# A long convolution before two feed-forward layers: spectrum of the signal channel-major, packed signal loads, complex product in fewer operations, b axis of 229 cells

## The chip, the cores and the metric

The kernel runs on one core of a Trainium2 chip. A core has a matrix engine (TensorE, PE in the rows; its weight loads are shown as PEld), three elementwise engines (VectorE, DVE; ScalarE, ACT; GpSimd, POOL) and a queue processor (SyncE, SP), which issues most transfers here. The engines run side by side, each in its own program order, and wait for each other at semaphores. SBUF and PSUM are the memories on the core; a transfer to or from main memory is a DMA. The metric is the device time of one execution in microseconds (us).

## What is computed

```python
h_mlp = np.maximum(pos_emb @ w1, 0.0) @ w2            # 12480 x 128, pos_emb 12480 x 64
h_filt = h_mlp * np.exp(-0.01 * pos)[:, None]
u = x * v                                             # 12480 x 128
L = 2 * S
Uf = np.fft.rfft(u, n=L, axis=1)
Hf = np.fft.rfft(h_filt, n=L, axis=0)
y = np.fft.irfft(Uf * Hf[None, :, :], n=L, axis=1)[:, :S, :]
out = x * y
# then two feed-forward layers, 128 -> 2048 -> 128, on every token:
#   out = square(relu(out @ w_in)) @ w_out
#   out = leaky(out @ w_in2, alpha) @ w_out2
```

S is 12480. All data are 32-bit floats; the weights of the feed-forward layers come as 64-bit words.

## The kernel before

**Index scheme.** The convolution is cyclic, over L = NA x NB = 110 x 227 cells. A position n is written as (a, b) with n = 227 a + 110 b modulo L, so that the Fourier transform falls into one over a (110 values) and one over b (227 values). Both are done as matmuls with tables. Since the signals are real, the a axis gives K2 = 112 rows (cosine and sine of 56 frequencies). On the b axis only 114 columns are kept (HB): b and -b are held side by side and folded into a sum (even part) and a difference (odd part).

**Stages.** Each is a Python generator; `run` interleaves two of them by weights, and every engine executes its own instructions in the order in which they were written. The order is set by hand (`manual_schedule`).

1. `z_stage` and `ar_stage` (L155, L187): filter. Position embeddings are multiplied by w1, windowed, and transformed over a (result `ar`).
2. `u_stage(0)` beside `r_stage` (L333, L207). `r_stage` transforms the filter over b in 28 steps and spills it to main memory, in pieces `r`. `u_stage` treats the 128 channels of the signal in 32 blocks of four (16 for each half h = 0, 1): load x and v, multiply (`mul_xv`, POOL, L247), in seven blocks fold on POOL (L263, L264), transform over a (`u_mm_a`, L273) and, one step later, over b (`u_mm_b`). In half 0 the operands of the b transform are split into a high and a low part, and each product is three matmuls (`mm_b`, L309); in half 1 it is one (L305; an instruction of this kind on 32-bit floats stands twice in the trace). The halves' results are the spectra U.
3. `u_stage(1)` beside `p_stage(0)` (called p0). `p_stage` has 14 steps for each half. A step loads a piece `r`, multiplies it by w2 into the banks H (L384), and forms the complex product with U: four multiplications and a subtraction on DVE (L389, L395) into a buffer T (two in a ring), an addition on POOL (L361) or, in eight of 28 steps, on DVE (L397), and then, one step late (`finish`, L358), the sum and the difference of two channel halves, written back over U on POOL (L364; once for each half on DVE).
4. `p_stage(1)` (called q0) beside `b_stage(0)`; then `b_stage(1)` alone, beside 60 steps that decode feed-forward weights. `b_stage` transforms back over b: per channel one matmul with a column of U as stationary operand (L410), per four channels a copy on ACT (L416) into `gv`.
5. `y_stage` (L427): back over a, multiplied by x; 30 column groups; beside it goes the decoding of weights.
6. `moe` (L614): both feed-forward layers in 25 chunks of up to 500 columns.

**Layout.** U of half 0 lies in the upper halves of the rows of a large buffer G, U of half 1 in R2: `uview` (L114) gives [114 partitions, 112 frequencies k, 128 channels x], with the channels contiguous. So a column of U for one channel (`U[:, :, x]`, L410) steps over 256 floats in G and 128 in R2. The rings for x (eight), v (two) and intermediate results lie in the lower halves of G's rows. x and v are loaded with both signs of b, 110 x 8 x 128 floats a block each (440 KB), `load_x` and `load_v` on SP's queue.

**Order on the queues.** POOL executes, in the order written, per step of u_stage `mul_xv(k + 4)`, `fold(k + 2)`, per step of p_stage the additions and `finish` of the step before. SP issues the loads of x and v, the spills and loads of `r`, the loads of x for y_stage and the weight words, in the order written.

## Time and profile before

| | |
|---|---|
| runs, us | 1514.84, 1514.22, 1513.73 (median 1514.22) |
| span of the profiled execution, us | 1510.0 |
| instructions | 23069 |
| TensorE busy, share of the span | 98% |
| DVE, ACT, POOL busy | 78%, 65%, 59% |
| mean granted TensorE clock | 0.993 |
| moved by DMA | 83.38 MB |

The span runs from the first to the last instruction of the profiled execution; its time outside the span is not recorded, and the runs' median is 4.2 us longer than the span. Busy shares are means over stages with different limits, and a busy TensorE is not one at its peak, since its matmuls are pipelined and their ends are modelled. So a stage is read from its own window: which engine is busy throughout, which waits end last, and how fast the instructions follow each other in the chain.

### The profile page before, as it was taken

Reading aid. Unit: us, or ns where it says so; the run is one execution under the profiler, and the core shown is the slowest. Engines: PE = TensorE matmul, PEld = TensorE weight load, DVE = VectorE, ACT = ScalarE, POOL = GpSimd, SP = SyncE. Lnnn points to the kernel's source line nnn. Section 1 sums busy time; section 2 is a strip of 40 time slices with the busy share of each in tenths; the row PEclk is TensorE's granted clock in tenths of the full one; section 3 lists DMA queues with packets and bytes.
Section 4 is the critical chain, followed back from the end, with each engine's and each line's share of the span. In section 5 each row is a group of like instructions: output and inputs, shape, how many; then the busy total and the mean of one; then the engine's idle time right before and its main releaser. Section 6 shows DMA issues by size and latency. Waiting matters only on the chain.

```text
span 1510.0 us, 23069 instructions
## 1 busy us (share of the span) xinstructions
PE 1476.9 (98%) x7676; PEld 1276.9 (85%) x7676; DVE 1177.1 (78%) x1898; ACT 978.8 (65%) x1887; POOL 898.0 (59%) x808
## 2 busy tenths in 40 slices
PE   8998799999999999999999999999999999999998
PEld 8987689999988888888888888888888888888887
DVE  5987998745878877777777777777777777777998
ACT  5353122243288877777777777777777777777776
POOL 0575886623476666656666666566666656665564
PEclk9998999999999999999999999999999999999999
DMA  8788862224940000000000000000000000000000
GB/s 256 176 241 228 203 168 62 77 52 120 278 134 22 1 1 8 8 8 8 7 1 7 8 7 8 7 8 8 0 8 8 7 8 8 8 1 7 15 14 14
DMA packets 86082, 83.38 MB, mean 55 GB/s; under 512 B 5642, under 2 KB 77642, under 8 KB 85578
## 3 DMA queue, kind: packets, MB, share of 16 engines
q1 hardware_dynamic: 84865, 77.68, 18.5%
q0 software_dynamic: 688, 3.93, 0.8%
q8 instruction: 60, 0.98, 0.3%
q14 instruction: 60, 0.49, 0.1%
q10 hardware_dynamic: 409, 0.29, 0.1%
HBM read 65.03 MB, written 16.86 MB: 54 GB/s over the span
## 4 chain that ended last, share of the span: by engine, by line
PE 88%; DMA 7%; DVE 2%; POOL 2%; issue 1%; ACT 0%; SPq 0%; POOLq 0%; DVEq 0%; ACTq 0%
PE bank L621 24%; PE bank L620 24%; PE bank L622 24%; PE bank L410 7%; DMA G<-in_vs_dram 3%; PE bank L384 3%; DMA r<-spill 3%; PE bank L461 2%; PE bank L460 2%; DVE R L197 2%; PE bank L273 1%; DMA G<-in_pos_dram 1%; POOL G L247 1%; PE bank L305 1%; PE bank L162 1%
## 5 line engine op out<-in xcount | busy, mean ns | idle before, releaser
L673 POOL TENSOR_TENSOR g<-R,g 128x500 fp32r<-128x500 f32 (+1 forms) x598 | 641.6, 1087 | 412.3 <-ACT g L662 306.5
L655 DVE SCALAR_TENSOR_TENSOR R<-bank,e 128x500 f32<-128x500 f32 (+1 forms) x800 | 527.3, 673 | 159.1 <-ACT e L643 118.7
L662 ACT CAST g<-R 128x500 fp32r<-128x500 f32 (+1 forms) x800 | 461.8, 604 | 15.9 <-DVE R L655 13.6
L640 ACT ACTIVATE e<-bank 128x500 f32<-128x500 f32 (+1 forms) x400 | 235.2, 588 | 176.1 <-PE bank L622 174.9
L645 DVE TENSOR_SCALAR e<-bank,alpha 128x500 f32<-128x500 f32 (+1 forms) x266 | 195.6, 735 | 68.5 <-PE bank L622 65.8
L621 PE MATMUL bank<-g,w_o 128*128 128x500 f32 (+1 forms) x400 | 155.5, 389 | 0.2 <-POOL g L673 0.2
L621 PE MATMUL bank<-x,w_i 128*128 128x500 f32 (+1 forms) x400 | 155.4, 389 | 0.0
L622 PE MATMUL bank<-g,w_o 128*128 128x500 f32 (+1 forms) x400 | 155.2, 388 | 0.0
L622 PE MATMUL bank<-x,w_i 128*128 128x500 f32 (+1 forms) x400 | 155.1, 388 | 0.0
L620 PE MATMUL bank<-x,w_i 128*128 128x500 f32 (+1 forms) x400 | 155.0, 388 | 0.0
L620 PE MATMUL bank<-g,w_o 128*128 128x500 f32 (+1 forms) x400 | 154.9, 387 | 0.0
L673 DVE TENSOR_TENSOR g<-R,g 128x500 fp32r<-128x500 f32 (+1 forms) x202 | 149.5, 740 | 0.3 <-ACT g L662 0.3
L621 PE MATMUL bank<-g,w_o0b 128*128 128x500 f32 (+1 forms) x350 | 136.3, 389 | 0.0
L620 PE MATMUL bank<-g,w_o0b 128*128 128x500 f32 (+1 forms) x350 | 135.4, 387 | 0.0
L622 PE MATMUL bank<-g,w_o0b 128*128 128x500 f32 (+1 forms) x350 | 135.3, 387 | 0.0
L247 POOL TENSOR_TENSOR G<-G 110x912 f32<-110x912 f32 x32 | 68.7, 2149 | 81.8 <-DMA G<-in_vs_dram 71.9
L642 ACT ACTIVATE e<-bank 128x500 f32<-128x500 f32 (+1 forms) x134 | 79.1, 590 | 46.2 <-PE bank L622 46.1
L643 ACT ACTIVATE e<-e,alpha 128x500 f32<-128x500 f32 (+1 forms) x134 | 95.6, 714 | 4.4
L416 ACT COPY G<-bank 112x456 f32<-112x456 f32 x63 | 33.9, 539 | 85.3 <-PE bank L410 85.3
L620 PEld LDWEIGHTS bank<-x,w_i 128*128 128x128 f32 x400 | 75.1, 188 | 15.8
L621 PEld LDWEIGHTS bank<-g,w_o 128*128 128x128 f32 x400 | 75.2, 188 | 15.7 <-POOL g L673 0.6
L620 PEld LDWEIGHTS bank<-g,w_o 128*128 128x128 f32 x400 | 75.2, 188 | 15.5
(141 smaller groups left out, 2802.9 us busy)
## 6 DMA issues: line engine op xcount, KB each, us to landing
G<-in_xs_dram SPq DMA_DIRECT2D x32, 440.0 KB
...
```

The costliest lines, as they stand in the source:

```text
L247: nc.gpsimd.tensor_tensor(out=x, in0=x, in1=v, op=ALU.mult)
L410: nc.tensor.matmul(p[:, d], lhsT=U[:, :, e * DH + g * DG + d], rhs=icosb if e == 0 else sinb)
L620: nc.tensor.matmul(p, lhsT=wl, rhs=xh, start=first, stop=False)
L621: nc.tensor.matmul(p, lhsT=wh, rhs=xl, start=False, stop=False)
L622: nc.tensor.matmul(p, lhsT=wh, rhs=xh, start=False, stop=last)
L640: nc.scalar.activation(out=r, in_=p, func=ACTF.Relu)
L642: nc.scalar.activation(out=r, in_=p, func=ACTF.Relu, scale=-1.0)
L643: nc.scalar.activation(out=r, in_=r, func=ACTF.Copy, scale=alpha[:, t:t + 1])
L645: nc.vector.tensor_scalar(out=r, in0=p, scalar1=0.0, scalar2=alpha[:, t:t + 1], op0=ALU.min, op1=ALU.mult)
L655: nc.vector.scalar_tensor_tensor(out=g, in0=p, scalar=0.0, in1=r, op0=ALU.max, op1=op)
L662: nc.scalar.copy(out=gh, in_=g)
L673: eng.tensor_tensor(out=gl, in0=g, in1=gh.bitcast(F32), op=ALU.subtract)
```

## The change

- The b axis has 229 cells (L = 110 x 229), 115 columns are kept, tables have 116. With this number no cell is taken by both signs of b.
- x and v are loaded packed: one array of 112 x 4 x 128 floats a block each (229 KB), in which cells of positive b lie forward and cells of negative b backward. `prep` (POOL) multiplies x by v and then takes the positive part out with a mask (`plus`); `minus` (POOL) subtracts it and reads the rest back to front. Rings: seven for x and v, three for the negative part.
- `u_mm_a` always folds after the transform; the split into high and low parts is gone in both halves; the frequency axis is ordered with cosine and sine alternating (c fastest).
- U is kept with the channels slow and the 112 frequencies contiguous. U of half 0 lies in two pieces (16 channels in the lower halves of G's rows, 112 in the upper).
- In `p_stage` a bank H holds [channel, sign, q, r]; one multiplication (two in half 0, by the pieces) forms U times H for both parts by reading H twice over, into T = (A, B); A of the real part minus B on DVE; A of the imaginary part plus B on POOL, in all steps; then sum and difference on POOL.
- `b_stage` reads a channel's 112 frequencies contiguously.
- Output and y_stage have exactly 12480 columns; four small tables move to the pool `late`, and `xt_first` to the pool `wo`.

```diff
 
 S, D, F, FF = 12480, 128, 64, 2048
-NA, NB = 110, 227
...
 K2 = 2 * KA
 HB = (NB + 1) // 2
-HP = HB // 2
+HP = -(-HB // 2)
+HX = 2 * HP
 KP = KA // 2
...
+    def U(h, x0, n):
+        if h:
+            return R2[:HB].rearrange("p (x k) -> p x k", k=K2)[:, x0:x0 + n]
+        if x0 < XF:
+            return gap[0][:HB, x0:x0 + n, 128 - K2:128]
+        return gap[1][:HB, x0 - XF:x0 - XF + n, 0:K2]
+
+    def parts(h):
+        return [(0, D)] if h else [(0, XF), (XF, D - XF)]
+
+    NX, NM = 7, 3
+    at = [XF]
+
+    def rows(n):
+        at[0] += n
+        assert at[0] <= HX
+        return gap[0][:, at[0] - n:at[0]]
+
+    m_ring = [rows(DG)[:, :, 0:HB] for _ in range(NM)]
+    a_ring = [rows(2 * DG)[:, :, 0:K2] for _ in range(2)]
+    ap_ring = [rows(DG)[:, :, 0:K2] for _ in range(2)]
+    t_ring = [rows(DG)[:, :, 0:K2] if i else gap[1][:, D - XF:D - XF + DG, 0:K2] for i in range(2)]
+    assert at[0] <= HP
+    at[0] = HP
+    x_ring = [[rows(DG) for _ in range(2)] for _ in range(NX)]
...
             if g in z_loads:
-                load_x(z_loads[g][0])
-                load_v(z_loads[g][1])
+                load(z_loads[g])
+                prep(z_loads[g] - 1)
...
+    z_loads = {5: 0, 10: 1, 15: 2, 19: 3, 24: 4, 28: 5}
...
-                    nc.tensor.matmul(p[s][:, j], lhsT=rv[:, f0 + j, :, s], rhs=dfa)
+                    nc.tensor.matmul(p[s][:, j], lhsT=rv[:, f0 + j, :, s], rhs=dfa_f)
...
+            load(NX - 1)
+            prep(NX - 2)
...
-    def load_x(n):
+    loaded, ready = [0], [0]
+
+    def load(n):
         while loaded[0] <= min(n, 2 * NG - 1):
             k = loaded[0]
-            nc.sync.dma_start(out=x_ring[k % NX][:NA], in_=xs[:, k])
+            for t, src in zip(x_ring[k % NX], (xs, vs)):
+                nc.sync.dma_start(out=t[:NAP], in_=src[:, k])
             loaded[0] += 1
 
-    def load_v(n):
-        while loaded[1] <= min(n, 2 * NG - 1):
-            k = loaded[1]
-            if k >= NV:
-                mul_xv(k - NV)
-            nc.sync.dma_start(out=v_ring[k % NV][:NA], in_=vs[:, k])
-            loaded[1] += 1
-
-    def mul_xv(n):
-        while mulled[0] <= min(n, 2 * NG - 1):
-            k = mulled[0]
-            x, v = x_ring[k % NX][:NA, :, 0:HB], v_ring[k % NV][:NA, :, 0:HB]
+    def prep(n):
+        while ready[0] <= min(n, 2 * NG - 1):
+            k = ready[0]
+            x, v = (t[:NA] for t in x_ring[k % NX])
+            x, v = x[:, :, 0:W], v[:, :, 0:W]
+            m = plus.unsqueeze(1).to_broadcast([NA, DG, W])
             nc.gpsimd.tensor_tensor(out=x, in0=x, in1=v, op=ALU.mult)
-            mulled[0] += 1
-
-    z_loads = {0: (0, -1), 6: (0, 0), 11: (1, 0), 15: (1, 1), 20: (2, 2), 25: (3, 3), 28: (4, 4)}
+            nc.gpsimd.tensor_tensor(out=v, in0=x, in1=m, op=ALU.mult)
+            ready[0] += 1
+
+    def minus(k):
+        if k < 2 * NG:
+            x, v = (back_to_front(t[:NA]) for t in x_ring[k % NX])
+            nc.gpsimd.tensor_tensor(out=m_ring[k % NM][:NA], in0=x, in1=v, op=ALU.subtract)
+
+    def back_to_front(t):
+        v = t[:, :, 1:W]
+        st = [list(x) for x in v.ap]
+        st[-1][0] = -st[-1][0]
+        return bass.AP(tensor=v.tensor, offset=v.offset + HB - 1, ap=st)
...
     def u_mm_a(k):
-        x = x_ring[k % NX].rearrange("p (d s) b -> p s d b", s=2)[:NA, :, :, 0:HB]
-        ap = ap_ring[k % 2]
+        u = x_ring[k % NX][1][:NA, :, 0:HB], m_ring[k % NM][:NA]
...
-                nc.tensor.matmul(p[s][:, d], lhsT=lhs[:, d], rhs=dfa)
...
-        ap = ap[:HB, :, 0:K2]
-        nc.scalar.copy(out=ap, in_=p[0])
-        dst = [p[e] if split and lo_engine(k, e) is nc.vector else a[:, e] for e in range(2)]
...
+                nc.tensor.matmul(p[s][:, d], lhsT=u[s][:, d], rhs=dfa)
+        a = a_t[k] = a_ring[k % 2][:HB].rearrange("p (e d) k -> p e d k", e=2)
+        t = ap_ring[k % 2][:HB]
+        nc.scalar.copy(out=t, in_=p[0])
...
+            nc.vector.tensor_tensor(out=a[:, e], in0=t, in1=p[1], op=op)
...
     def u_mm_b(k):
         h, g = divmod(k, NG)
-        U = uview(h)
         a = a_t.pop(k)
         po = bank(r_b, HB, DG, 2, KA)
-        pe = bank(r_b, HB, DG, 2, KA)
-        mm_b(po[:, :, 0], "nsin", a, 1, slice(KA, K2))
-        mm_b(po[:, :, 1], "sin", a, 1, slice(0, KA))
-        t = t_ring[k % 2][:HB, :, 0:K2]
-        nc.scalar.copy(out=t, in_=po.rearrange("p d c k -> p d (c k)"))
-        mm_b(pe.rearrange("p d c k -> p d (c k)"), "cos", a, 0, slice(0, K2))
+        pe = bank(r_b, HB, DG, K2)
+        ao = a[:, 1].rearrange("p d (k c) -> p d k c", c=2)
+        nc.tensor.matmul(po[:, :, 0], lhsT=nsinb, rhs=ao[:, :, :, 1])
+        nc.tensor.matmul(po[:, :, 1], lhsT=sinb, rhs=ao[:, :, :, 0])
+        t = t_ring[k % 2][:HB]
+        nc.scalar.copy(out=t.rearrange("p d (k c) -> p d k c", c=2), in_=po.rearrange("p d c k -> p d k c"))
+        nc.tensor.matmul(pe, lhsT=cosb, rhs=a[:, 0])
+        u = U(h, 2 * DG * g, 2 * DG).rearrange("p (d s) k -> p d s k", s=2)
         for s, op in ((0, ALU.add), (1, ALU.subtract)):
-            x0 = s * DH + g * DG
-            nc.vector.tensor_tensor(
-                out=U[:, :, x0:x0 + DG],
-                in0=pe.rearrange("p d c k -> p (c k) d"),
-                in1=t.rearrange("p d k -> p k d"),
-                op=op,
-            )
+            nc.vector.tensor_tensor(out=u[:, :, s], in0=pe, in1=t, op=op)
 
     def u_stage(h):
         for k in range(h * NG, (h + 1) * NG + 1):
             if k == 0:
-                fold(0)
-                fold(1)
+                minus(0)
+                minus(1)
             if k < (h + 1) * NG:
-                load_x(k + NX - 1)
-                load_v(k + min(NX, XE + 1 + k) - 1)
-                mul_xv(k + 4)
+                load(k + NX - 1)
                 u_mm_a(k)
-                fold(k + 2)
+                minus(k + 2)
+                prep(k + NX - 3)
             if k > h * NG:
                 u_mm_b(k - 1)
             yield
 
     nj = KP // 2
-    add_dve = {nj - 1} | set(range(nj + 1, 2 * nj, 2))
     p_order = [(j + nj - 3) % nj for j in range(nj)]
     p_order += [(j + nj - 6) % nj for j in range(nj)]
 
     def p_stage(h, t_ring, r_ring):
-        U = uview(h)
-        Uc = U.rearrange("p (c k) x -> p c k x", c=2)
         late = []
 
-        def finish(n, j, T):
+        def finish(n, j, A, B):
             last = n % nj == nj - 1
-            if n not in add_dve:
-                nc.gpsimd.tensor_tensor(out=T[:, 1], in0=T[:, 1], in1=T[:, 2], op=ALU.add)
-            for s, op in ((0, ALU.add), (1, ALU.subtract)):
-                eng = nc.vector if last and s == 0 else nc.gpsimd
-                eng.tensor_tensor(
-                    out=Uc[:, :, 4 * j:4 * j + 4, s * DH:(s + 1) * DH],
-                    in0=T[:, 0:2, :, 0],
-                    in1=T[:, 0:2, :, 1],
-                    op=op,
-                )
+            nc.gpsimd.tensor_tensor(out=A[:, :, :, 1], in0=A[:, :, :, 1], in1=B[:, :, :, 0], op=ALU.add)
+            for x0, m in parts(h):
+                y = A[:, x0:x0 + m].rearrange("p (d s) k c -> p d s (k c)", s=2)
+                u = U(h, x0, m).rearrange("p (d s) k -> p d s k", s=2)[:, :, :, 8 * j:8 * j + 8]
+                for s, op in ((0, ALU.add), (1, ALU.subtract)):
+                    eng = nc.vector if last and s == 0 else nc.gpsimd
+                    eng.tensor_tensor(out=u[:, :, s], in0=y[:, :, 0], in1=y[:, :, 1], op=op)
...
-            H = [bank(r_h, HB, 2, 2, 2, DH) for c in range(2)]
             T = t_ring()
             for c in range(2):
-                for s in range(2):
-                    for q in range(2):
+                H = bank(r_h, HB, DH, 2, 2, 2)
+                for q in range(2):
+                    for s in range(2):
                         nc.tensor.matmul(
-                            H[c][:, s, q], lhsT=r[:, q, 2 * s + c], rhs=w2_sb[:, h * 2 * DH:(h + 1) * 2 * DH]
+                            H[:, :, s, q], lhsT=r[:, q, 2 * s + c], rhs=w2_sb[:, h * D:(h + 1) * D]
                         )
-                hv = H[c].rearrange("p s q r d -> p (q r) s d")
-                for uc in range(2):
+                hv = H.rearrange("p d s q r -> p (d s) (q r)")
+                for x0, m in parts(h):
                     nc.vector.tensor_tensor(
-                        out=hv if uc * c else T[:, uc + c + (uc > c)],
-                        in0=U[:, uc * KA + 4 * j:uc * KA + 4 * j + 4].rearrange("p k (s d) -> p k s d", s=2),
-                        in1=hv,
+                        out=T[:, c, x0:x0 + m],
+                        in0=U(h, x0, m)[:, :, 8 * j:8 * j + 8].rearrange("p x (k c) -> p x k c", c=2),
+                        in1=hv[:, x0:x0 + m].unsqueeze(3).to_broadcast([HB, m, 4, 2]),
                         op=ALU.mult,
                     )
-            nc.vector.tensor_tensor(out=T[:, 0], in0=T[:, 0], in1=hv, op=ALU.subtract)
-            if n in add_dve:
-                nc.vector.tensor_tensor(out=T[:, 1], in0=T[:, 1], in1=T[:, 2], op=ALU.add)
+            A, B = T[:, 0], T[:, 1]
+            nc.vector.tensor_tensor(out=A[:, :, :, 0], in0=A[:, :, :, 0], in1=B[:, :, :, 1], op=ALU.subtract)
             if late:
                 late.pop()()
-            late.append(lambda n=n, j=j, T=T: finish(n, j, T))
+            late.append(lambda n=n, j=j, A=A, B=B: finish(n, j, A, B))
...
-                p = bank(r_y if alone else r_ab, K2, DG, HB)
+                p = bank(r_y if alone else r_ab, K2, DG, HX)
                 for d in range(DG):
-                    nc.tensor.matmul(p[:, d], lhsT=U[:, :, e * DH + g * DG + d], rhs=icosb if e == 0 else sinb)
+                    nc.tensor.matmul(
+                        p[:, d], lhsT=U(h, 2 * (g * DG + d) + e, 1)[:, 0], rhs=icosb if e == 0 else isinb
+                    )
...
             late = st.enter_context(tc.tile_pool(name="late", bufs=1))
+            w2_sb = late.tile([128, 2 * D], F32, name="w2_sb")
+            dfa = late.tile([NA, K2], F32, name="dfa")
+            dfa_f = late.tile([NA, K2], F32, name="dfa_f")
+            plus = late.tile([NA, W], F32, name="plus")
...
+            with tc.tile_pool(name="rt", bufs=1) as rt:
+                run((u_stage(0), NG + 1), (r_stage(rt, r_ring), KP))
             big = st.enter_context(tc.tile_pool(name="tt", bufs=1))
-            tt = ring_of(big, 2, [HB, 3, 4, 2, DH], F32, "T")
+            tt = ring_of(big, 2, [HB, 2, D, 4, 2], F32, "T")
             p0, q0 = p_stage(0, tt, r_ring), p_stage(1, tt, r_ring)
             run((u_stage(1), NG + 1), (p0, nj + 1))
...
-        ys = y_stage(wst.tile([128, 3 * HA], F32, name="xt_first"))
-        next(ys)
         with tc.tile_pool(name="wo", bufs=1) as wo:
+            ys = y_stage(wo.tile([128, 3 * HA], F32, name="xt_first"))
+            next(ys)
...
+    packed = np.full((NAP, 128), S)
+    packed[:NA, :HB] = np.where(live[:, :, 0], n[:, :, 0], S)
+    turned, there = n[:, :0:-1, 1], live[:, :0:-1, 1]
+    assert not (live[:, 1:, 0] & there).any()
+    packed[:NA, 1:HB] = np.where(there, turned, packed[:NA, 1:HB])
+    plus = np.zeros((NA, W), np.float32)
+    plus[:, :HB] = live[:, :, 0]
+
     def sig(x):
-        c = np.zeros((NA, D, 2, 128), x.dtype)
-        c[..., :HB] = cells(x).transpose(0, 3, 2, 1)
-        return c.reshape(NA, D // DG, DG * 2, 128)
+        c = np.concatenate([x, np.zeros((1, x.shape[1]), x.dtype)])[packed]
+        return np.ascontiguousarray(c.transpose(0, 2, 1)).reshape(NAP, D // DG, DG, 128)
```

## Rows read from the trace of the kernel before

**Rows 1.** The page: the chain that ended last, by line

```profile
PE bank L621 24%; PE bank L620 24%; PE bank L622 24%; PE bank L410 7%; DMA G<-in_vs_dram 3%; PE bank L384 3%; DMA r<-spill 3%; PE bank L461 2%; PE bank L460 2%; DVE R L197 2%; PE bank L273 1%; DMA G<-in_pos_dram 1%; POOL G L247 1%; PE bank L305 1%; PE bank L162 1%
```

**Rows 2.** Windows by stage: length, busy us (instructions), granted clock, DMA share, GB/s

```profile
62.00:149.30 87.30, 77.37 (x626) 74.08 (x627) 71.06 (x135) 40.67 (x91) 54.60 (x34) 0.94 0.85 229
149.30:240.60 91.30, 79.46 (x577) 69.99 (x576) 86.05 (x131) 17.57 (x33) 76.51 (x55) 0.96 0.66 161
240.60:314.20 73.60, 73.60 (x465) 73.60 (x466) 50.99 (x80) 16.72 (x31) 43.37 (x34) 0.98 0.25 72
314.20:364.20 50.00, 49.54 (x259) 49.41 (x258) 18.12 (x43) 22.38 (x49) 11.68 (x16) 1.00 0.18 54
364.20:418.70 54.50, 54.42 (x457) 53.99 (x457) 46.81 (x111) 11.63 (x32) 24.64 (x34) 1.00 0.90 267
418.70:1510.00 1091.30, 1086.28 (x4798) 900.14 (x4797) 857.68 (x1350) 842.74 (x1558) 672.62 (x625) 1.00 0.03 12
```

**Rows 3.** Lines by form on POOL, 62 to 149.3 us

```profile
L247 POOL TENSOR_TENSOR G<-G 110x912 f32<-110x912 f32 x17 | 36.6, 2150 | 32.5 <-DMA G<-in_vs_dram 28.3 <-PE bank L213 3.9
```

**Rows 4.** The chain in order of time: start us, us, what (instructions)

```profile
65.90 1.24 PE bank L309 x9
...
75.46 1.79 PE bank L213 x16
...
197.87 1.60 PE bank L273 x16
199.46 1.51 PE bank L305 x6
...
220.47 1.75 PE bank L384 x16
...
252.07 3.07 PE bank L410 x16
```

**Rows 5.** Lines by form, first 430 us, weight loads: busy us, mean ns

```profile
L273 PEld LDWEIGHTS bank<-dfa,G 110*114 110x114 f32 x512 | 57.4, 189 | 1.1 <-issue 0.7 <-DVE a_lo L284 0.2 <-POOL G L364 0.2
...
L410 PEld LDWEIGHTS bank<-dfb,G 114*112 114x112 f32 x256 | 50.3, 285 | 2.2 <-issue 2.2
...
L460 PEld LDWEIGHTS bank<-ide,G 112*128 112x128 f32 x228 | 35.8, 196 | 0.0
```

**Rows 6.** Lines by form on POOL, 149.3 to 240.6 us

```profile
L364 POOL TENSOR_TENSOR G<-T 114x512 f32<-114x512 f32 x27 | 33.9, 1276 | 2.5 <-DVE T L397 1.5
L247 POOL TENSOR_TENSOR G<-G 110x912 f32<-110x912 f32 x11 | 23.6, 2144 | 14.4 <-DMA G<-in_vs_dram 12.1 <-PE bank L305 2.2
...
L264 POOL TENSOR_TENSOR G<-G 110x456 f32<-110x456 f32 x2 | 2.3, 1166 | 0.2
```

**Rows 7.** Lines by form, first 430 us: elementwise prices

```profile
L416 ACT COPY G<-bank 112x456 f32<-112x456 f32 x63 | 33.9, 539 | 85.3 <-PE bank L410 85.3
...
L326 DVE TENSOR_TENSOR R<-bank,G 114x448 f32<-114x448 f32 x32 | 28.7, 938 | 0.8 <-PE bank L305 0.7
...
L389 DVE TENSOR_TENSOR T<-R,bank 114x512 f32<-114x512 f32 x42 | 26.4, 682 | 16.7 <-PE bank L384 16.6
...
L290 DVE TENSOR_TENSOR G<-G,bank 114x448 f32<-114x448 f32 x38 | 22.1, 613 | 3.5 <-PE bank L273 1.9 <-POOL G L263 1.6
```

**Rows 8.** Timeline, 306 to 312 us: start us, us, instruction

```profile
308.10 0.69 DVE L364 TENSOR_TENSOR R<-T 114x512 f32<-114x512 f32 x1
...
308.15 1.78 POOL L364 TENSOR_TENSOR R<-T 114x512 f32<-114x512 f32 x1 [2.81 <-DVE T L397]
```

**Rows 9.** Timeline, 62 us

```profile
61.79 1.17 POOL L264 TENSOR_TENSOR G<-G 110x456 f32<-110x456 f32 x1
...
62.33 0.76 DVE L743 TENSOR_TENSOR cos_lo<-dfb,cos_hi 114x114 fp32r<-114x114 f32 x1 [0.40 <-ACT cos_hi L742]
...
63.01 0.26 DVE L743 TENSOR_TENSOR sin_lo<-dfb,sin_hi 114x114 fp32r<-114x114 f32 x1
```

**Rows 10.** Lines by form on POOL, 418.7 to 1510 us

```profile
L673 POOL TENSOR_TENSOR g<-R,g 128x500 fp32r<-128x500 f32 x572 | 614.7, 1088 | 388.0 <-ACT g L662 286.3 <-PE bank L620 85.5 <-PE bank L622 14.3
```

More of the change, by code (lines that the diff above doesn't have):

```diff
@@ L66 @@
     win: bass.AP,
+    live: bass.AP,
     dft_a: bass.AP,
@@ L133 @@
-    for i in range(2):
-        a_ring.append(rows(2 * DG))
-        ap_ring.append(rows(DG))
-        t_ring.append(rows(DG))
+    def U(h, x0, n):
[12 more added lines that the diff above has]
+        return gap[0][:, at[0] - n:at[0]]
@@ L296, in u_mm_a @@
-        a_t[k] = split[k % len(split)] if split else (a,)
-    split, tabs = [], {}
-    def lo_engine(k, e):
-        return nc.vector if e or k < 3 else nc.gpsimd
-    def mm_b(out, name, a, e, cols):
-        if len(a) == 1:
-            nc.tensor.matmul(out, lhsT=dfb[:, TAB[name]], rhs=a[0][:, e, :, cols])
-            return
-        th, tl = tabs[name]
-        for i, (t, x) in enumerate(((tl, a[0]), (th, a[1]), (th, a[0]))):
-            nc.tensor.matmul(out, lhsT=t, rhs=x[:, e, :, cols], start=i == 0, stop=i == 2)
@@ L917 @@
     got = r.results[0]["out_0_dram"].T
-    keep = order < S
     y = np.empty((S, D), got.dtype)
-    y[order[keep]] = got[:order.size][keep]
+    y[order] = got
     return y
```

138 lines of the change are left out of this document (46 added, 92 removed).

## The prediction

> **What bounds the kernel now.** I read the page's chain by line first, then a table of windows cut where the chain changes line, then the chain row by row in each window, then the lines of the engine that ends it. The three matmul lines of the two feed-forward layers hold 71% of the chain [rows 1]; that part lasts 1091.3 us of 1510.0 [rows 2] and the change touches it only through a last chunk of 480 columns for 486: 192 matmuls by 6 columns at 2.4 GHz, 0.5 us less. The rest, 418.7 us, is the convolution, in stages that I call by their generators: filter (0 to 62 us), u0 with r (87.3), u1 with p0 (91.3), q0 with b0 (73.6), b1 (50.0), y (54.5) [rows 2]. Each has its own limit:
> - u0 waits for x and v: DMA share 0.85 at 229 GB/s, and the multiplication on POOL sat 28.3 us waiting for v [rows 2, 3].
> - u1/p0 has two limits close together: POOL is busy 76.5 of 91.3 us, DVE 86.1 [rows 2].
> - q0/b0 and b1 are TensorE throughout (73.6 of 73.6, 49.5 of 50.0) [rows 2]. There 16 instructions of L410 take 3.07 us where 16 of L273, of nearly the same size, take 1.60 [rows 4]. The reason stands in the weight loads: L410 loads 112 columns in 285 ns, L273 114 columns in 189 ns [rows 5]. L410's stationary operand steps 1024 bytes from element to element (512 in b1), L273's lies contiguous. A step of 8 bytes (L460) costs nothing that the row shows: 196 ns for 128 columns [rows 5].
> - y is TensorE too, and little in it changes.
>
> The profiled execution has a span of 1510.0 us; the median of the runs is 4.2 us above it, which I take as what lies around the span, and add at the end.
>
> **Filter stage.** Four small tables more lie on SP's queue behind the position loads, which are issued first. Position loads grow by 1% (115 columns for 114), signal loads halve and come later. I take 0, between -1 and +1.
>
> **u0 with r.** A block of four channels now brings 2 x 229 KB in place of 2 x 451 KB. The stage moves 15 blocks (6.9 MB) and 14 spills of 0.47 MB (6.6 MB), 13.5 MB; at the 229 GB/s of the row [rows 2] that is 59 us. So DMA stops being the limit, and TensorE is next. The split into high and low parts is gone, so the b transform takes 1.51 us (L305) in place of 1.24 (L309) [rows 4]. Sum: 16 x (1.60 + 1.51) + 28 x 1.79/2 = 74.8 us [rows 4]. DVE needs 39 us for its 64 operations of 0.613 [rows 7] and some 22 for r, and POOL 54 us by the prices below: both less. On SP a load now waits for the transform of the block six before it, a step earlier in TensorE's order, and the spills queue behind it without loss. I take 77, two for start and end. **-10 us.** Unknown: the odd matmuls read their moving operand at 8-byte steps. The nearest rows are L460, at the same step and without a cost [rows 5], and L410, 3.07 us for 1.60, 1.9 times [rows 4]; that factor on half of 1.51 us, 16 times, makes 0 to +11 us. The step is L460's, so I take 0.
>
> **POOL, the term that decides.** All prices come from two rows: 456 columns 1.166 us, 912 columns 2.144 us [rows 6], so 0.19 us and 2.145 ns a column; 512 columns are a row of their own, 1.276 us.
> - Each block had one multiplication of 912 columns, and seven of the 32 had two folds of 456 besides. Now each has x*v and the mask (464 columns, 1.18 us each) and a reversed subtraction (460 columns, 1.18 us): 3.55 us in place of 2.15.
> - Each step of p0 had two or three operations of 512 columns. Now it has one of 512 and, because this half lies in two pieces of 16 and 112 channels, two of 64 and two of 448: 1.276 + 2 x (0.325 + 1.149) = 4.22 us. In q0 it has three of 512: 3.83 us, where half the additions were on DVE.
>
> When u1 begins, POOL has been given masks up to block 19 and reversals up to block 17. For u1 with p0 there remain 12 x 2.37 + 14 x 1.18 + 14 x 4.22, less 1.47 for the half that DVE does in the last step: 102.5 us. The same stage needs 16 x 3.11 + 14 x 1.75 = 74.3 us of TensorE [rows 4], and of DVE 39.2 us (four operations of 0.613 a block: the strided write of 0.94 goes [rows 7]) + 14 x 3.42 = 87 us. (448 columns take DVE 0.613 us and 512 take 0.682 [rows 7], so 896 take 1.10 and 128 take 0.27; a step of p0 is two products in these two pieces and one subtraction of 512.) So POOL ends last, and it is behind POOL that the queues form: a block's first transform waits for its reversal, and DVE's next product waits for a T buffer that POOL's finish frees (two buffers).
>
> **The lock.** DVE's subtraction A - B now has both inputs in SBUF, in each of 28 steps, while POOL has no gaps. Two places show what that does. At 308 us DVE's L364 (two SBUF inputs, 0.69 us) ran beside POOL's L364, which took 1.78 us in place of 1.276: +0.50 [rows 6, 8]. At 62 us it went the other way: DVE's L743 took 0.76 us in place of 0.26 while POOL was at work [rows 9]. I charge POOL 0.50 a step, 14 x 0.5 = 7 us for each half; the ends are 0 and the whole 0.69 (28 steps: 0 to 19 us). The Trainium skill ("SBUF — State Buffer", Who interferes with whom) says that a DVE instruction with two SBUF inputs contends with a GpSimd one that reads SBUF, and that the first to issue decides who waits. By that rule the other engine loses the whole instruction, 0.69 us, and the sum below would be 1490; by the row, 0.50, it is 1485.
>
> u1 with p0: 102.5 + 7, of which some 2 us fall into the end of u0: 108 us where it was 91.3. **+17 us.** TensorE idles a third of it in gaps of about 3 us; before, in this window, it also had gaps and a granted clock of 0.96 [rows 2], and with 34 us in hand a lower clock costs nothing until it is below two thirds.
>
> **q0 with b0.** The weights are contiguous now, so 16 instructions of the inverse take the 1.60 us of L273, not 3.07 [rows 4]: TensorE needs 16 x 1.60 + 14 x 1.75 = 50 us. POOL needs 14 x 3.83 - 1.28 + 7 = 59 us and ends last: 60 us for 73.6. **-14 us.** Unknown: H is written to PSUM in pairs, one pair in 32 bytes. No row has such a write; strided PSUM operands of DVE cost 0.94 for 0.61 us (L326 beside L290) [rows 7], and weight loads 1.9 times [rows 4]. At 1.9 times TensorE needs 25.6 + 46.6 = 72 us here: 0 to +12. I take 0, since pairs stay whole.
>
> **b1.** 16 x 1.60 = 25.6 us of TensorE. Beside it lie 32 copies on ACT (539 ns each, L416 [rows 7]) and 60 steps of weight decoding, in all 22.4 us of ACT and 18.1 of DVE [rows 2]. They fit, though narrowly, and ACT also waits in order for the first weights and for DVE. I take 28, between 26 and 34. **-22 us.**
>
> **y** (its first tile moves to another pool, opened at the same point of the program, so its load waits for the same end of q0) gains one column group and has one term more: +0.5. The sum is 62 + 77 + 108 + 60 + 28 + 55 + 1090.8 = 1480.8, plus 4.2 around the span: **1485 us**, 29 below.
>
> **The rivals.**
> - *POOL is cheaper than I priced it*, for lack of the lock (-14) or by its rate: in the feed-forward part it does 500 columns in 1.088 us (L673 [rows 10]), 13% under these rows. With either, 1464 to 1474. Against it: all rows of the stages themselves agree on the dearer rate. Chance 0.21.
> - *Strided writes of H (and strided moving reads) slow TensorE*: +12 in q0 and up to +11 in u0, 1497 to 1508. The Trainium skill ("PSUM — Partial Sum Buffer", Specifications) says that any non-contiguous access to PSUM slows matmuls significantly. No row here shows a strided write. Chance 0.11.
> - *Slower: POOL pays for short runs.* Its new operations read with 8-byte steps (the addition), in runs of eight elements (the finish), or backwards; every POOL row here reads runs of 64 and more. One mechanism, in p0 and q0, where POOL ends last. At the 1.53 times that strides cost DVE [rows 7], the finishes' 58 + 52 us grow by 58, and the time is 1540. It decides from 1.27 times on, where the 29 us are gone. For it: nothing in the trace excludes it. Against it: DVE's price is for steps of 448 bytes. The Trainium skill ("GPSIMD Engine Reference", Performance pitfalls for Q7 kernels) puts the cliff at steps above 8 bytes, so these would just escape; no run here shows it. Chance 0.14.
> - *Weight loads do not get faster*, because the step was not their reason: the inverses stay at 3.07 us, q0/b0 at 74 and b1 at 50: 1521. L273 speaks against it. Chance 0.03.
>
> **How the numbers follow.** The forecast, 1476 to 1496 with its own unknowns, has 0.47; 0.04 remain for what I do not see, half of it near no change. A measurement here tells about 0.2% (3 us) from nothing. Faster: 0.47 + 0.21 + 0.11 + 0.01 = 0.80. Same: 0.03 (the edge of the slow rivals among it). Slower: 0.17. The range leaves the slow rivals out above and the cheapest POOL (no lock and the low rate together) below: 1462 to 1512.
>
> **What would show it.** Right: L410's successor at about 0.1 us an instruction; DMA share under 0.75 in u0; POOL busy over 0.9 from the start of u1 to the start of b1, with idle time on TensorE put down to POOL; POOL rows beside DVE's subtraction longer by about 0.5 us; b1 under 30 us. Wrong: POOL operations over 1.3 us at 448 to 512 columns (slow rival) or near 1.1 (cheap one); H matmuls above 1.75 us for 16; a b1 that ACT ends.

## The result, and the profile after

The changed kernel takes 1487.51 us (median of four runs, 1486.9 to 1488.09); the kernel before took 1513.97 beside it (1513.4 to 1514.84). The ratio is 0.9831, with a 95% interval of 0.9817 to 0.9845: 26 us faster, where 1485 was predicted. The profiled execution has a span of 1485.1 us.

The stages of the changed kernel, as windows cut at the same places as [rows 2] (length, busy us and instructions of PE, PEld, DVE, ACT and POOL, granted clock, DMA share, GB/s); in order filter, u0, u1/p0, q0/b0, b1, y, feed-forward:

```profile
0.00:62.90 62.90, 56.99 (x502) 56.61 (x502) 46.39 (x52) 28.04 (x96) 18.02 (x20) 1.00 0.63 174
62.90:138.50 75.60, 75.58 (x577) 67.96 (x578) 56.36 (x120) 26.90 (x60) 52.88 (x46) 1.00 0.59 170
138.50:246.00 107.50, 84.55 (x579) 72.83 (x578) 99.12 (x137) 16.51 (x31) 103.38 (x103) 0.92 0.41 96
246.00:309.20 63.20, 50.86 (x466) 48.69 (x465) 46.13 (x43) 17.48 (x32) 60.00 (x41) 1.00 0.27 83
309.20:336.50 27.30, 27.28 (x257) 27.13 (x257) 17.43 (x41) 20.26 (x48) 12.68 (x17) 0.94 0.41 102
336.50:392.20 55.70, 55.40 (x464) 55.14 (x465) 47.68 (x111) 11.68 (x32) 24.29 (x33) 1.00 0.88 264
392.20:1485.10 1092.90, 1087.85 (x4797) 900.52 (x4795) 862.78 (x1350) 846.04 (x1558) 808.92 (x626) 1.00 0.03 12
```

In the second row TensorE is busy for the whole length (75.58 of 75.60), and the DMA share is 0.59; in the third and fourth POOL comes nearest to the length (103.38 of 107.50, 60.00 of 63.20), and TensorE idles. Beside the prediction (lengths in us):

| stage | before | predicted | after | after minus predicted |
|---|---|---|---|---|
| filter | 62.0 | 62 | 62.9 | +0.9 |
| u0 | 87.3 | 77 | 75.6 | -1.4 |
| u1/p0 | 91.3 | 108 | 107.5 | -0.5 |
| q0/b0 | 73.6 | 60 | 63.2 | +3.2 |
| b1 | 50.0 | 28 | 27.3 | -0.7 |
| y | 54.5 | 55 | 55.7 | +0.7 |
| feed-forward | 1091.3 | 1090.8 | 1092.9 | +2.1 |
| outside the span | 4.2 | 4.2 | 2.4 | -1.8 |

The last row is the median of the runs less the span of the one profiled execution. Every run of either kernel whose span is on record is about 1.8 us longer than that span (1486.9 for 1485.1). So some 2.4 of the 4.2 and 0.6 of the 2.4 lie between executions, not around the span.

The chain that ended last, in order of time (start us, us, what): TensorE at the start of u1/p0, one step of p0 beside u1, then one of q0.

```profile
148.46 1.75 PE bank L342 x16
...
157.09 1.20 DVE T L347 x2
...
158.30 1.17 POOL G L255
159.47 1.45 POOL T L321
...
161.00 3.10 POOL G L327 x4
...
164.13 2.29 DVE T L347 x3
```

```profile
262.08 1.51 POOL T L321
...
263.66 1.86 POOL R L327 x2
265.52 1.03 issue
```

L255 is the mask, L321 the addition, L327 the finish, L347 DVE's product, L342 the matmuls that write H. From 157 to 236 us a step of p0 is closed by POOL handing a T buffer to DVE and DVE handing it back, as the prediction had it. From the start of the stage to 154 us the chain is TensorE's, one instruction behind the other, and in the last 10 us of the stage it runs through the end of u1 on DVE and TensorE. In q0 the chain is POOL alone (two finishes take 2.94 us on POOL there; the row gives part of them as issue).

POOL's lines by form (busy us, mean ns | idle before):

```profile
L631 POOL TENSOR_TENSOR g<-R,g 128x500 fp32r<-128x500 f32 x572 | 744.5, 1323 | 261.4 <-ACT g L620 189.0 <-PE bank L578 61.4 <-PE bank L580 8.5
L321 POOL TENSOR_TENSOR T<-T 115x512 f32<-115x512 f32 x28 | 43.0, 1535 | 4.0 <-DVE T L347 3.9
L327 POOL TENSOR_TENSOR R<-T 115x512 f32<-115x512 f32 x27 | 40.0, 1502 | 1.1
L254 POOL TENSOR_TENSOR G<-G 110x464 f32<-110x464 f32 x32 | 38.0, 1186 | 26.2 <-DMA G<-in_xs_dram 26.2
...
L261 POOL TENSOR_TENSOR G<-G 110x460 f32<-110x460 f32 x32 | 37.4, 1170 | 39.7 <-PE bank L276 36.2 <-issue 2.3 <-PE bank L203 1.2
...
L327 POOL TENSOR_TENSOR G<-T 115x448 f32<-115x448 f32 x27 | 31.2, 1175 | 0.0
...
L327 POOL TENSOR_TENSOR G<-T 115x64 f32<-115x64 f32 x27 | 11.4, 440 | 1.1
```

L254 (x times v), the mask L255 (1.174 us) and the reversed L261 cost what 2.145 ns a column gives. L321 does not: 1.535 us for 512 columns, where [rows 6] has 1.276. Nor does the first row, the low part of the feed-forward operands, whose code the change does not touch: 500 columns take 1.323 us where [rows 10] has 1.088.

### The profile page after: what moved, and what is told of

It reads as the page before. It is cut to its first block, busy times and chain, and to the rows that moved or that the text cites. A ratio compares the mean times of both kernels' runs of the same rounds, so it can differ in the third digit from the quotient of the medians.

```text
span 1485.1 us, 23021 instructions
## 1 busy us (share of the span) xinstructions
PE 1438.5 (97%) x7634; PEld 1228.9 (83%) x7634; DVE 1175.9 (79%) x1852; ACT 966.9 (65%) x1857; POOL 1080.2 (73%) x883
## 4 chain that ended last, share of the span: by engine, by line
PE 86%; POOL 8%; DVE 4%; issue 2%; ACT 0%; DMA 0%; POOLq 0%; DVEq 0%; ACTq 0%
PE bank L578 24%; PE bank L579 24%; PE bank L580 24%; POOL T L321 2%; POOL G L327 2%; PE bank L276 2%; PE bank L170 2%; PE bank L420 2%; PE bank L366 2%; PE bank L419 2%; DVE R L207 2%; PE bank L225 2%; POOL R L327 2%; DVE T L347 1%; PE bank L293 1%
## 5 line engine op out<-in xcount | busy, mean ns | idle before, releaser
L631 POOL TENSOR_TENSOR g<-R,g 128x500 fp32r<-128x500 f32 (+1 forms) x598 | 777.5, 1322 | 277.9 <-ACT g L620 202.0
L631 DVE TENSOR_TENSOR g<-R,g 128x500 fp32r<-128x500 f32 (+1 forms) x202 | 154.5, 765 | 0.0
L579 PEld LDWEIGHTS bank<-x,w_i 128*128 128x128 f32 x400 | 75.1, 188 | 15.9
L578 PEld LDWEIGHTS bank<-x,w_i 128*128 128x128 f32 x400 | 75.3, 188 | 15.6
L580 PEld LDWEIGHTS bank<-x,w_i 128*128 128x128 f32 x400 | 75.1, 188 | 15.3
```

Source lines behind the costliest of these rows:

```text
L578: nc.tensor.matmul(p, lhsT=wl, rhs=xh, start=first, stop=False)
L579: nc.tensor.matmul(p, lhsT=wh, rhs=xl, start=False, stop=False)
L580: nc.tensor.matmul(p, lhsT=wh, rhs=xh, start=False, stop=last)
L631: eng.tensor_tensor(out=gl, in0=g, in1=gh.bitcast(F32), op=ALU.subtract)
```

## Experiments

Each is one edit of the changed kernel (e, f) or of the kernel before (b).

**e1: the inverse reads strided weights again.**

```diff
-    p[:, d], lhsT=U(h, 2 * (g * DG + d) + e, 1)[:, 0], ...
+    p[:, d], lhsT=old(h, 2 * (g * DG + d) + e), ...
+def old(h, x):
+    if h: return R2[:HB].rearrange("p (k x) -> p k x", x=128)[:, :, x]
+    return gap[1][:HB, 0:K2, min(x, K2 - 1)]
```

> The changed kernel, but the inverse transform reads its stationary operand as the kernel before did (1024 bytes from element to element in the first half, 512 in the second). It takes other elements than the right ones; number, size and order of the instructions stay. If contiguous weight loads are what shortened q0/b0 and b1: weight loads go from 0.18 us back to about 0.285, 16 of these matmuls take 3.07 us again, b1 goes from 28 to about 50, q0/b0 from 63 to about 74 (14 x 1.75 + 16 x 3.07 on TensorE, which again ends last there), and the total is about 1520. If something else shortened them (the layout of what is written, the order, the clock): both stages stay within 2 us and the total is about 1487.

1517.72 us in one run. Weight loads of the inverse (ns min/median/max, first and last start us), first of e1, then of the changed kernel:

```profile
L371 PEld LDWEIGHTS bank<-dfb,G x256: 264/285/287, 245.7 to 317.3; 115*112 115x112 f32 x128
L371 PEld LDWEIGHTS bank<-dfb,R x256: 283/285/287, 317.5 to 366.5; 115*112 115x112 f32 x128
```

```profile
L366 PEld LDWEIGHTS bank<-dfb,G x256: 174/177/179, 245.9 to 304.8; 115*112 115x112 f32 x128
L366 PEld LDWEIGHTS bank<-dfb,R x256: 177/177/312, 309.2 to 336.1; 115*112 115x112 f32 x128
```

q0/b0 takes 71.7 us and b1 49.3, TensorE busy throughout. So the contiguous column of U is what shortened both; 30 us hang on it. The step of 512 bytes (R) costs as much as that of 1024 (G).

**e2: no DVE operation of p0 and q0 with two SBUF inputs.**

```diff
+ # second product: one half to T, the other in place in PSUM
+ nc.vector.tensor_tensor(out=T[:, c, x0:x0 + m, :, 0], in0=u[:, :, :, 0], in1=v, op=ALU.mult)
+ nc.vector.tensor_tensor(out=v, in0=u[:, :, :, 1], in1=v, op=ALU.mult)
- nc.vector.tensor_tensor(out=A[..., 0], in0=A[..., 0], in1=B[..., 1], op=ALU.subtract)
+ nc.vector.tensor_tensor(out=A[..., 0], in0=A[..., 0], in1=hv, op=ALU.subtract)
```

> The changed kernel, but the half of the second product that the subtraction needs is written into the PSUM bank of H in place, so that DVE's subtraction has one input in SBUF and one in PSUM; no DVE operation of p0 and q0 then has both inputs in SBUF. DVE does one operation more per step (+0.15 us), results are the same. Theory (POOL pays for DVE's subtraction only where its operations run without gaps): the second of POOL's finishing operations in q0 goes from 1.71 to 1.26 us, q0/b0 from 63.3 to about 57, p0 hardly moves (its POOL rows are only 0.15 us a step above their price), DVE's subtraction goes from 2.09 us (p0) and 0.93 (q0) to about 0.7; total about 1480. Rival (the loser waits out the whole other instruction in each of the 28 steps, on POOL): about 1468 to 1474. Rival (the long rows are not a lock): POOL's rows stay and the total stays at 1487 to 1489.

1474.62 us, ratio to before 0.9734 (95% interval 0.9710 to 0.9758). u1/p0 is 102.5 us, q0/b0 56.2. DVE's subtraction and POOL's finish, in the changed kernel and then in e2 (by line: ns min/median/max; by form: busy us, mean ns | idle before):

```profile
L354 DVE TENSOR_TENSOR T<-T x28: 693/942/3157, 142.3 to 304.8; 115x512 f32<-115x512 f32 x28
...
L354 DVE TENSOR_TENSOR T<-T 115x512 f32<-115x512 f32 x28 | 42.1, 1505 | 1.0
```

```profile
L327 POOL TENSOR_TENSOR R<-T x27: 1259/1707/1761, 250.2 to 308.4; 115x512 f32<-115x512 f32 x27
```

```profile
L360 DVE TENSOR_TENSOR T<-T,bank 115x512 f32<-115x512 f32 x28 | 19.3, 689 | 1.0
```

```profile
L327 POOL TENSOR_TENSOR R<-T x27: 1257/1268/1762, 243.5 to 296.0; 115x512 f32<-115x512 f32 x27
```

The median of the finish in q0 falls from 1.707 to 1.268 us, and DVE's subtraction from a mean of 1.505 us to 0.689. So each engine held up the other: DVE lost 23 us (42.1 - 19.3), POOL 0.44 us a step of q0. The two stages lost 5.0 + 7.0 = 12 us, 0.43 a step. I had expected p0 hardly to move and a total of 1480; the 1474.62 lie nearer to the rival's 1468 to 1474. In p0 POOL's finishing operations had each lost a little too (64 columns from a mean of 0.440 us to 0.320, 448 from 1.175 to 1.141, 27 times each: 4.2 us).

**e3: the addition on contiguous elements; e5: the frequency axis in two halves.** In the second the addition reads runs of four, and all that is computed stays.

```diff
- ...tensor_tensor(out=A[:, :, :, 1], in0=A[:, :, :, 1], in1=B[:, :, :, 0], op=ALU.add)
+ ...tensor_tensor(out=A[:, 0:DH], in0=A[:, 0:DH], in1=B[:, 0:DH], op=ALU.add)     # e3
+ ...tensor_tensor(out=A[:, :, 1], in0=A[:, :, 1], in1=B[:, :, 0], op=ALU.add)     # e5
- tt = ring_of(big, 2, [HB, 2, D, 4, 2], F32, "T")
+ tt = ring_of(big, 2, [HB, 2, D, 2, 4], F32, "T")                                 # e5
```

> The changed kernel, but POOL's addition reads and writes 512 contiguous elements in place of every second one; it adds other elements than the right ones, everything else stays. If the 8-byte step is what makes this operation 1.49 us: it goes to 1.28, the two stages where POOL ends last get 14 x 0.21 us shorter each, total about 1481.5. If the operation is long because of what runs beside it (the lock, DVE's port): it stays at 1.49 and the total at 1487.

> The changed kernel with the frequency axis in two halves (all cosine parts, then all sine parts) in place of interleaved pairs, from the tables to the product; the same results. POOL's addition then reads runs of four elements with a step of eight in place of single elements with a step of two; its finish writes runs of four in place of eight, the b transform's odd matmuls read contiguous operands. If the 8-byte step alone makes the addition dear and runs of four are free: addition 1.49 to 1.28 us, total 1481 as with the contiguous addition. If POOL pays by the number of runs: the addition goes to about 1.35 or more and the finish gets dearer, total 1484 to 1495. If the odd matmuls paid for their 8-byte step, u0 falls below 75 us; if not it stays at 75.6.

e3 1480.06 us (ratio 0.9773, 0.9743 to 0.9802), e5 1479.97 (0.9758, 0.9714 to 0.9801). The addition in e3, then in e5 with the finish that writes runs of four:

```profile
L321 POOL TENSOR_TENSOR T<-T 115x512 f32<-115x512 f32 x28 | 35.6, 1270 | 4.2 <-DVE T L354 4.2
```

```profile
L327 POOL TENSOR_TENSOR R<-T 115x512 f32<-115x512 f32 x27 | 39.5, 1483 | 1.1
...
L321 POOL TENSOR_TENSOR T<-T 115x512 f32<-115x512 f32 x28 | 37.0, 1320 | 4.1 <-DVE T L347 4.0
```

Against a mean of 1.535 us in the changed kernel, the addition gets 0.22 (e5) to 0.27 us (e3) cheaper; runs of four cost nothing (the finish keeps its 1.48, which still holds the waits of e2). The lock is not the reason: in e2 the addition still takes 1.509. But the step of 8 bytes is not alone in going: the addition's inputs start 12 bytes apart modulo 16 in the changed kernel (B lies 4096 bytes behind A, and A is read from its second element), and 0 apart in e3 and e5. Which of the two made the price was not separated. Both stages get 3 to 4 us shorter; q0/b0 takes 60.4 us in e3 and 59.8 in e5. In e5 u0 falls from 75.6 to 74.8 us, as the odd matmuls (the sine tables of the b transform) go from 363 to 354 ns.

**e4: x and v fetched twice.**

```diff
+ for src in (xs, vs):
+     nc.sync.dma_start(out=more(), in_=src[:, k])   # until the end of u0; nobody reads it
```

> The changed kernel, but until the end of u0 each block of x and v is fetched a second time into a buffer that nobody reads, so that the bytes of the kernel before move again while all arithmetic stays as in the changed one. If halving the bytes is what took u0 from 87.3 to 75.7 us: 13.5 + 6.9 MB at the 229 GB/s of the kernel before take 89 us, u0 goes to 86 to 90, DMA share above 0.8, total about 1500. If u0 got shorter for another reason (no split of x, deeper ring, other POOL work): u0 stays at 76 to 78 and the total at 1487 to 1489.

1488.77 us in one run. u0 (columns as in the windows above):

```profile
62.80:138.40 75.60, 75.59 (x577) 67.97 (x578) 56.35 (x120) 26.90 (x60) 52.84 (x46) 1.00 0.95 261
```

19.7 MB move (261 GB/s for 75.6 us), where the kernel before moved 20.0 (229 for 87.3, [rows 2]), and u0 is not a tenth of a microsecond longer. My theory of the bytes falls: 229 GB/s was no ceiling. The second copies land in pieces of 2 KB, those of the kernel before in rows of 512 bytes, but that explains little: by an estimate from these rows, a share of 1 would be 269 GB/s in the kernel before (229 / 0.85) and 275 in e4 (261 / 0.95).

**b1 to b4: the kernel before, with one suspect of u0 taken away.**

```diff
- NX, NV = 8, 2
+ NX, NV = 7, 3                                     # b1, b3: three buffers for v
- XE = 5
+ XE = 4                                            # b3: and where they lie (and when three blocks are loaded)
- return nc.vector if e or k < 3 else nc.gpsimd
+ return nc.vector                                  # b2: low parts on DVE
+ split.clear()                                     # b4: u0 without the split
```

> The kernel before with three buffers for v in place of two (and seven for x in place of eight); nothing else. If u0 was bound by the bytes, as the prediction had it: DMA share and rate stay at 0.85 and 229 GB/s, u0 at 86 to 88 us, total 1514. If it was bound by the wait for one of two v buffers, each load starting only when POOL had freed one: POOL's waits for v fall from 28 us to under 10, the rate rises towards the 261 GB/s of the run with twofold loads, u0 goes to 76 to 80, total about 1505.

> The kernel before with all low parts of the a transform on DVE (11 of them were on POOL in u0); nothing else. If what cost u0 was that POOL's low part stood in order behind a multiplication that waited for v: TensorE's 21 us of waits for it go away and u0 goes to 77 to 81 us although the bytes and the waits for v stay as they were. If the bytes or the v buffers bound it: TensorE waits for the product in place of the low part, u0 at 86 to 88, total 1514.

> The kernel before with three buffers for v in place of two, all of them where its signal buffers lay before, and seven for x; the multiplication that frees a v buffer moves from five to three blocks ahead. If the bytes bound u0: 20 MB at 229 GB/s, u0 at 86 to 88 us, the share of DMA stays at 0.85, total 1514. If the two v buffers bound it: the share rises to 0.9 or more, POOL's waits for v fall from 28 us to under 12, u0 goes to 78 to 82, total 1505 to 1510 (u1 with p0 keeps its length).

> The kernel before with the split of the a transform's result into high and low parts left out in u0 (its b transforms run on the unsplit values, as in the changed kernel); loads, buffers and bytes as before; the same results. If bytes bound u0, through whichever buffer: TensorE waits for x times v at the a transform in place of the low part, 229 GB/s, u0 at 85 to 88 us. If the split bound it (the chain of ACT, DVE and POOL between the two transforms, with POOL's part queued behind a multiplication that waits for v): TensorE's waits for low parts are gone, its 74.8 us have no gaps, u0 goes to 76 to 79 us and the bytes move at 255 GB/s or so. In the run with the low parts on DVE the 6 us won in u0 were given back in u1/p0 (91 to 101 us), where TensorE waited for fetched spills: if the transfers are behind by bytes, the same is seen here, total 1510 to 1515; if not, total about 1504.

b1 took 1544.29 us and tells nothing of u0: its third buffer lay on filter values that were still needed, which spoiled them and made the filter stage 17 us longer. The others, one run each, took 1514.41 (b2), 1521.35 (b3) and 1520.06 us (b4). u0 and u1/p0 of b2, then b3, then b4:

```profile
63.00:143.90 80.90, 74.02 (x624) 71.50 (x625) 76.61 (x142) 39.57 (x91) 42.12 (x23) 0.98 0.86 229
143.90:244.50 100.60, 80.94 (x580) 71.13 (x578) 88.00 (x135) 17.60 (x34) 77.80 (x55) 0.93 0.67 159
```

```profile
61.60:149.60 88.00, 77.28 (x624) 73.61 (x625) 71.11 (x135) 40.56 (x91) 52.68 (x33) 0.95 0.85 227
149.60:250.80 101.20, 83.71 (x578) 74.24 (x576) 86.26 (x131) 17.56 (x33) 78.07 (x56) 0.91 0.66 151
```

```profile
62.40:146.10 83.70, 78.25 (x576) 70.31 (x577) 59.38 (x111) 30.38 (x69) 42.09 (x23) 0.96 0.85 223
146.10:249.50 103.40, 82.88 (x579) 73.25 (x577) 87.72 (x135) 17.57 (x33) 77.88 (x55) 0.90 0.69 154
```

DMA stays at 0.85 or 0.86 and 223 to 229 GB/s, whatever is taken away. Without POOL's low parts u0 wins 6.4 us (b2), without the split 3.6 (b4), and u1/p0 gives back 9.3 and 12.1: there TensorE waits for fetched pieces of the filter. The wait of b4 in u1/p0 (engine, line, waited for: us, times, longest; the kernel before has 9.8 us for it, b2 17.7):

```profile
PE bank L384 <- DMA r<-spill: 18.6, 5, 9.3
```

This points to the transfers as what set the pace of both stages of the kernel before, as their part of its chain says too [rows 1], though not by their bytes alone; it is argued, since no run freed them. What kept them at 0.85 is not settled; no single suspect did. u0 of b3 came out as expected if the bytes bound it, u0 of b2 as expected if POOL's order did, and u0 of b4 between its two expectations. The changed kernel's order of loads with unpacked signals was not tried.

**e7: two shifts of 8 bytes.**

```diff
- R2[:, NTOK + i * CH:NTOK + (i + 1) * CH]
+ R2[:, NTOK + 2 + i * CH:NTOK + 2 + (i + 1) * CH]
- x, v = x[:, :, 0:W], v[:, :, 0:W]
+ x, v = x[:, :, 0:W], v[:, :, 2:2 + W]
```

> The changed kernel with two shifts of 8 bytes and nothing else: v lies two elements further in its tiles (the table of positions is rolled by two), and the three buffers that the feed-forward part keeps behind the tokens start two elements later, as they did in the kernel before, where 12486 tokens lay ahead of them. Theory (POOL's rate with two inputs goes by where the inputs start relative to each other, modulo 16 bytes): the low part in the feed-forward goes from 1.275 us back to 1.08, with nothing gained in time there; x*v, with inputs 8 bytes apart now, goes from 1.17 to about 1.0 us, and u1/p0 gets about 2 us shorter: total 1485. Rival (the low part got slower for what runs beside it): both rows stay where they are, total 1487.

1483.87 us (ratio 0.9785, 0.9749 to 0.9821). L632 is the low part, L255 x times v, L262 the reversed subtraction, L256 the mask, whose inputs were not shifted against each other:

```profile
L632 POOL TENSOR_TENSOR g<-R,g 128x500 fp32r<-128x500 f32 x572 | 615.8, 1090 | 388.2 <-ACT g L621 287.0 <-PE bank L579 86.0 <-PE bank L581 13.2
...
L256 POOL TENSOR_TENSOR G<-G,plus 110x464 f32<-110x464 f32 x32 | 37.6, 1175 | 2.5
L255 POOL TENSOR_TENSOR G<-G 110x464 f32<-110x464 f32 x32 | 32.7, 1023 | 26.3 <-DMA G<-in_xs_dram 26.3
L262 POOL TENSOR_TENSOR G<-G 110x460 f32<-110x460 f32 x32 | 31.5, 984 | 46.0 <-PE bank L277 41.7 <-issue 2.7 <-PE bank L204 1.6
```

The low part is back at the price of [rows 10], and 744 us of POOL become 616; the feed-forward part, where POOL is not the bound, gets 0.9 us shorter (1092.0). A start 8 bytes apart makes x times v and the subtraction 14 to 16% cheaper too, and u1/p0 2.0 us shorter.

**f1 and f2: what helped, together.** f1 is e2, e5 and e7 in one. f2 gives POOL's other operations inputs 8 bytes apart as well:

```diff
- tt = ring_of(big, 2, [HB, 2, D, 2, 4], F32, "T")
+ tt = ring_of(big, 2, [HB, DH * 18 + 4 * D + 2], F32, "T")   # pairs in steps of 10 and 18; B two further
- plus = late.tile([NA, W], F32, name="plus")
+ plus = late.tile([NA, W + 2], F32, name="plus")[:, 2:]
```

> The changed kernel with the three edits that helped, together: no DVE operation with two SBUF inputs in p0 and q0, the frequency axis in two halves, the two shifts of 8 bytes; the same results. If POOL is what ends u1/p0 and q0/b0, its savings add up until DVE or TensorE is next: u1/p0 107.5 - 5.0 - 2.8 - 2.0 = 97.7, or less, down to 94 (DVE has 83 us of work there, TensorE 83), q0/b0 63.2 - 7.0 - 3.0 = 53 (TensorE has 50), total 1463 to 1467. If another engine is already next behind POOL, they do not add up: 1470 to 1474.

> As f1_all, and POOL's other operations (the mask, the addition, the two finishing operations) get inputs that lie 8 bytes apart modulo 16 too: the table of the mask starts two elements later, the product tile has steps of 10 and 18 elements in place of 8 and 16. DVE does one operation more per step, +0.15 us. If the relative start of the two inputs sets POOL's rate also for runs of four and eight: mask 1.17 to 1.01, addition 1.28 to 1.08 to 1.10, finish of 512 from 1.27 to 1.08 to 1.10; POOL's sum falls to about 90 us in u1/p0 and 46 in q0, where TensorE's 50 us end last then: u1/p0 91 to 94, q0/b0 51 to 52, total 1457 to 1460. If it does so only for long runs: as f1_all, or 2 to 4 us more for DVE.

f1 takes 1462.86 us (ratio to before 0.9661, 0.9637 to 0.9684), f2 1454.25 (0.9596, 0.9571 to 0.9620): the fastest of all. u1/p0 and q0/b0 of f2; the addition and the finish of f1; POOL's lines of f2; a step of q0 in its chain:

```profile
138.10:229.60 91.50, 80.55 (x578) 70.75 (x577) 83.80 (x193) 16.50 (x31) 83.53 (x103) 0.96 0.47 113
229.60:278.00 48.40, 48.33 (x467) 48.17 (x465) 44.82 (x71) 16.95 (x32) 45.45 (x41) 1.00 0.35 109
```

```profile
L322 POOL TENSOR_TENSOR T<-T 115x512 f32<-115x512 f32 x28 | 35.7, 1274 | 5.1 <-DVE T L358 5.1
L328 POOL TENSOR_TENSOR R<-T 115x512 f32<-115x512 f32 x27 | 34.1, 1285 | 1.1
```

```profile
L323 POOL TENSOR_TENSOR T<-T 115x512 f32<-115x512 f32 x28 | 32.9, 1176 | 7.4 <-DVE T L363 7.4
...
L256 POOL TENSOR_TENSOR G<-G,plus 110x464 f32<-110x464 f32 x32 | 32.3, 1009 | 2.5
...
L329 POOL TENSOR_TENSOR R<-T 115x512 f32<-115x512 f32 x27 | 30.4, 1148 | 1.2 <-DVE T L367 0.2
```

```profile
242.99 2.20 POOL R L329 x2
245.20 1.14 POOL T L323
```

The mask falls from 1.18 to 1.01 us, the finish from 1.285 to 1.148, the addition from 1.274 to 1.176. (In the finish and the mask the inputs lie 8 bytes apart in every run; in the addition their starts do, and from run to run the distance changes between 8 and 0.) In q0/b0 TensorE is now busy throughout (48.33 of 48.40), yet the chain there is still POOL's, 3.4 us a step. The savings added up: 107.5 less 5.0 (e2), 2.7 (e5) and 2.0 (e7) is 97.8 us for u1/p0, and f1 has 96.5; q0/b0 goes from 63.2 to 52.8 (f1) and 48.4 (f2).

## Why the prediction was right, point by point

- **b1 and half of q0/b0: contiguous weight loads.** Right, mechanism and size: 177 ns for 285 (e1), 27.3 us for b1.
- **POOL ends last in u1/p0 and q0/b0.** Right, in u1/p0 from 157 to 236 us. That u1/p0 is only 0.5 us from its forecast is partly luck: POOL is busy 103.4 us where the sum had 107.5 (109.5 less some 2 in u0), and idle for 4.1 that the sum did not have; and the addition, 2.7 to 4.1 us too cheap in the sum (e5, e3), meets a lock charged 2.0 too high (e2). TensorE, at a granted clock of 0.92, idles there.
- **The lock.** Right in size, half right in place. I charged POOL 0.50 us a step; e2 shows 12 us over 28 steps, 0.43. It fell on POOL in q0. In p0 it fell above all on DVE, whose subtraction took up to 3.16 us; of the 5.0 us that the stage lost, 4.2 were POOL's own. The Trainium skill ("SBUF — State Buffer", Who interferes with whom) has the loser wait out the other instruction. For DVE it was more: the subtraction that starts at 166.45 us lasts through two POOL operations in a row, the mask and the addition, which ends at 169.05 (start us, us, instruction):

```profile
166.43 1.17 POOL L255 TENSOR_TENSOR G<-G,plus 110x464 f32<-110x464 f32 x1
166.45 3.14 DVE L354 TENSOR_TENSOR T<-T 115x512 f32<-115x512 f32 x1
...
167.56 1.49 POOL L321 TENSOR_TENSOR T<-T 115x512 f32<-115x512 f32 x1
```

  For POOL it was less: 0.44 where DVE's whole instruction is 0.69. What the stages lost is nearer to the row's 0.50.
- **q0/b0: the term that was mis-sized.** Its 3.2 us too many are POOL's addition. I priced it by contiguous columns, 1.276 us; in q0 it takes about 1.50, and 14 times 0.22 is 3.1 us. With it at 1.27 or 1.32 the stage takes 60.4 or 59.8 us (e3, e5), the forecast's 60. The mechanism of the slow rival (short runs, 8-byte steps, backwards) thus shows in at most one of its three forms: 1.16 to 1.21 times on the addition (its inputs' starts changed with the step), nothing for runs of eight (448 columns 1.13 to 1.18 us), of four, or backwards (460 columns 1.17). The sign that the prediction named against itself, over 1.3 us at 448 to 512 columns, did appear, on the addition and, by the lock, on the finish of q0; with the deciding point at 1.27 on the finishes, the rival stayed far from deciding. The Trainium skill ("GPSIMD Engine Reference", Performance pitfalls for Q7 kernels) puts the cliff at steps above 8 bytes; the addition, at a step of 8, was 1.21 times as dear as in e3, and whether the step or the inputs' starts made it so is open.
- **u0: the right time, by a step that failed.** TensorE's sum (74.8, measured 75.6) is what ends it, as predicted. That halved bytes lift the limit is not: e4 moves the old amount in the same time. 229 GB/s was no ceiling. What the runs leave, argued and not shown, is that in the kernel before the order of loads and waits on SP's queue made the transfers the bound over u0 and u1/p0 together (178.6 us, and 181.5 to 189.2 in b2 to b4).
- **The unknowns taken as zero.** Strided moving operands cost 9 ns an instruction of 354, 0.6 us for the 64 of u0, which gets 0.8 us shorter without them (e5). H's strided writes cost nothing: 16 of them take 1.75 us as in [rows 4]. The Trainium skill ("PSUM — Partial Sum Buffer", Specifications) has any non-contiguous access slow matmuls significantly; for pairs within 32 bytes that is not seen here.
- **POOL is cheaper than priced.** The cheap rate of [rows 10] is real and a matter of addresses (e7), not of the stage. The changed kernel's tiles did not have it, so the rival failed; f2 shows what it was worth once they have.
- **Feed-forward, +2.1 us.** I forecast 0.5 us less. The low part got 21% dearer by the same addresses, 12480 tokens lying ahead of its buffers in place of 12486; undoing that gives 0.9 us (e7). The rest is not explained. It and the q0/b0 miss are offset by u0, b1 and the 1.8 us by which the last row of the table differs, which is a matter of the executions profiled and not of the change. So part of the total's nearness (1487.5 for 1485) is luck.
